# One semaphore or two for the turns of two kinds of products in a packed TensorE stream

## The chip, the cores and the metric

The kernel runs on one core of a Trainium2 chip. The metric is the device time of one execution in microseconds; three runs of the kernel before took 1469.01, 1470.53 and 1471.32 us, median 1470.53.

## The reference

Attention and a dense MLP work in parallel on the same normalised input, and both are added to the input. S = 2048 rows, D = 512, 32 heads of 16, F = 1792, all in f32.

```python
xn = _layernorm(x, axis=-1)
q, k, v = split(xn @ wqkv)                       # 32 heads of 16
p = softmax(einsum("bhqd,bhkd->bhqk", q, k) * 16 ** -0.5)
a = einsum("bhqk,bhkd->bhqd", p, v) -> (S, D) @ wo
m = gelu(xn @ w1 + b1) @ w2 + b2
out = x + a + m
```

## The kernel before, in words

**Units.** The attention is cut into 32 tasks (8 groups of 4 heads times 4 blocks of 512 queries) of 16 units each, 512 units in all. A unit does four score tiles twice: once as S, 128 queries by 512 keys, of which VectorE takes the row maxima (`s_half`, the `reduce_max` in line 366, tiles `pS`), and 19 units later (`LEAD`) once as T, 128 keys by 512 queries (`e_half`, tiles `pT`), of which ScalarE takes the exponentials (line 414, `pe<-pT`). The products of the exponentials with v (`v_half`, tiles `pV`, f32) follow one or two units behind. They add up over the 16 units of a task in one PSUM bank. A column of ones in v gives the softmax's sums.

**Dense work.** The projections of q, k and v, the MLP and the output projection are cut into groups (class `Group`), whose products add up in one PSUM bank too (tiles `pD`). f32 values are split into two f16 halves, and each product is made of three f16 products. `unit` takes from the current group a fixed number of them per half unit (`dense`): the pace (4, 4), (3, 4) or (3, 3), for even and odd units. The first MLP layer has 56 groups of 12 products on each side, (3, 3) for even and (4, 4) for odd f; the second has 16 groups of 42 products on each side, (3, 4) for the first eight and (4, 4) for the others. All else has (4, 4).

**Packing.** Scores, v products and dense products contract over at most 64 rows, and each is issued as four products of 64 rows by 32 columns. Such a product uses one of eight tiles of the TensorE array: one of two sides (partitions 0 to 63 or 64 to 127) and one of four columns of 32. I call four products that fill one side a set. Sets on the two sides run at the same time. Two sets that add up into one bank must not, so that V and D each change sides from half unit to half unit: where V is on one side, D is on the other, and in the next half unit they change places.

**The order of a half unit**, called a block here, is written out in `unit`: T, S, S, T (two on each side), then V (one set), then 3 or 4 sets of D, all on the other side than V. Only in the first block of a task D stands ahead of V. There are 1024 blocks with V. All instructions are issued in that order, with the manual schedule of line 863.

**Turns.** V of a block adds into the bank that V of the block before wrote from the other side, and so does D. To keep them apart, the last V product and the last D product of a block each count up a semaphore when they end (`leave`), unless their bank is finished with them. The first counted product of the next block waits for it (`enter` and `product`): V as a rule, since it stands ahead of D.

**Other waits** on TensorE: T waits until ScalarE has emptied its bank (three banks and one more shared with D), S until VectorE has (three banks), and a D product for its operands' DMA or for the GELU.

Of the kernel before, what the change touches and what calls it, by code (L numbers as in the profile page):

```python
# [54 lines left out]
def layer_kernel(ctx: ExitStack, tc: tile.TileContext, x, wqkv, wo, w1, b1, w2, b2, out):  # L55
# [63 lines left out]
    turn = [0]  # L119
# [41 lines left out]

    turns = tc.alloc_semaphore("turns")
    counted, left, newest, goal = [0], [], {}, [None]

    def product(user, *args, **kw):

        p = nc.tensor.matmul(*args, **kw)  # L169
        if user is None:  # L170
            return
        if goal[0] is not None:
            p._wait_ge(turns, counted[0])
            tc.declare_fence(p.ins, group=goal[0])
            goal[0] = None
        newest[user] = p

    def leave(user, goes_on):

        p = newest.pop(user, None)  # L180
        if p is not None and goes_on:
            p.then_inc(turns, 1)
            tc.no_tile_sem_insts.add(p.ins.name)
            counted[0] += 1
            left.append(p)

    def enter():

        if left:
            goal[0] = f"turn{counted[0]}"  # L190
            for p in left:
                tc.add_to_no_dep_group(goal[0], p.ins)
            left.clear()

    def tiled(user, dst, lhs, rhs, start, stop):

        for j in range(0, P, 32):
            product(user, dst[j:j + 32], lhs[:, j:j + 32], rhs, start=start, stop=stop)
# [218 lines left out]
    def v_half(u, a):  # L417

        t, kt = divmod(u, 16)
        g, qb = divmod(t, NQB)  # L420
        if kt == 0 and a == 0:
            pv_of[t] = hold("V", "S")
        pv = pv_of[t][0]
        r = slice(64 * a, 64 * a + 64)
        for h in (2, 3, 0, 1):
            c = (4 * g + h) * VW
            product("V", pv[32 * h:32 * h + 32, :], vv[r, kt, c:c + 32], ptiles[u, h][r],
                    start=(kt == 0 and a == 0), stop=(kt == 15 and a == 1))
# [321 lines left out]
    def land():  # L750

        settle()
        while extra[0] is not None:
            for side in range(2):
                if extra[0] is not None:
                    spare(None, side)
        if cur[0] is not None:
            enter()
        for side in range(2):
            while cur[0] is not None and cur[0].left(side):  # L760
                nc.tensor.drain()
                while cur[0].left(side):
                    cur[0].product(side)
        ended()

    def unit(gen):
# [7 lines left out]
        for a in range(2):  # L774
# [7 lines left out]
            if e >= 0:  # L782
                one_more()
                enter()

                w, r = (e - 2, 1) if a == 0 else (e - 1, 0)
                live = 0 <= w < NU
                new = r == 0 and w % 16 == 0
                if live and not new:
                    v_half(w, r)  # L790
                dense(gen, 1 - r)
                if live and new:
                    v_half(w, r)

                for user, goes_on in (("V", live and not (r == 1 and w % 16 == 15)),
                                      ("D", cur[0] is not None and not cur[0].over())):
                    leave(user, goes_on)
                for k in backlog:
                    backlog[k] = max(0, backlog[k] - HALF)
                if live and r == 1:  # L800
                    v_end(w)
                ended(False)
# [715 lines left out]
```

## Time and profile before

| | |
|---|---|
| median of three runs | 1470.53 us |
| the profiled execution, from first to last instruction | 1469.7 us |
| instructions | 88685, of them 40184 matmul records on TensorE |
| TensorE busy (any tile) | 1451.6 us, 99% |
| VectorE busy | 1368.7 us, 93% |
| ScalarE busy | 1259.3 us, 86% |
| GpSimd busy | 664.1 us, 45% |
| granted TensorE clock, mean | 0.996 |

Of the profiled execution no other time is given than its span; the median of the runs is 0.8 us above it. Times in the listings are microseconds. A timeline row gives start, duration, engine, line, operation, the tiles written and read, shapes and a count; rows of equal instructions that follow closely are merged, and the duration is then that of all of them. A row of a group gives the count, the busy time, the mean in ns of one, and the engine's idle time before them. An f32 product on TensorE stands in the trace as two records, one after the other. TensorE's matmul rows have modelled ends.

### The profile page before, as it was taken

What the parts mean: (1) busy time and instruction counts of PE and PEld (TensorE: products, weight loads), DVE (VectorE), ACT (ScalarE), POOL (GpSimd) and SP (SyncE); (2) the same over time, 40 slices, a digit from 0 to 9 for tenths busy, and PEclk for the clock granted to TensorE, in tenths of its full rate; (3) what the DMA queues carried; (4) which work ended last, traced back from release to release, by engine and by line L of the source; (5) the groups of instructions that cost most, each with busy time, mean ns of one, the idle gap of its engine ahead of it and who ended that gap; (6) DMA issues with size and microseconds to landing.
All of it is one profiled execution on the core that took longest, in us unless ns stands there. A gap on an engine that the chain in (4) does not pass through costs nothing.

```text
span 1469.7 us, 88685 instructions
## 1 busy us (share of the span) xinstructions
PE 1451.6 (99%) x40184; PEld 838.7 (57%) x40184; DVE 1368.7 (93%) x2304; ACT 1259.3 (86%) x2367; POOL 664.1 (45%) x673
## 2 busy tenths in 40 slices
PE   7999999999999999999999999999999999999998
PEld 3446556565565555556555556565555656555554
DVE  6989999999999999999999999999999999999933
ACT  5868888888999888899988889998889999888885
POOL 3201857554778411288740138883105777121110
PEclk9999999999999999999999999999999999999999
DMA  6731465455224211221113011121112210121423
GB/s 212 222 124 54 147 200 179 146 177 151 83 69 130 65 32 29 59 71 42 44 44 87 25 43 44 46 82 44 44 37 70 61 38 20 52 61 46 128 73 117
DMA packets 112627, 124.86 MB, mean 85 GB/s; under 512 B 22908, under 2 KB 84220, under 8 KB 112248
## 3 DMA queue, kind: packets, MB, share of 16 engines
q1 hardware_dynamic: 112248, 119.18, 26.6%
q8 instruction: 314, 5.14, 1.4%
q14 instruction: 65, 0.53, 0.1%
HBM read 81.66 MB, written 37.34 MB: 81 GB/s over the span
## 4 chain that ended last, share of the span: by engine, by line
PE 95%; DVE 2%; ACT 1%; DMA 1%; issue 1%; SPq 0%; DVEq 0%; ACTq 0%
PE pV L169 28%; PE pD L169 27%; PE pT L169 20%; PE pS L169 18%; PE pT L1015 2%; DMA wq<-in_A_wqkv_dram 1%; DVE mt L366 1%; PE pD L1015 1%; ACT xs L968 0%; ACT pe L414 0%; DVE ac L1393 0%; ACT wqk_h L904 0%; DVE xt L998 0%; DMA out_dram<-ac 0%; PE pT L985 0%
## 5 line engine op out<-in xcount | busy, mean ns | idle before, releaser
L366 DVE TENSOR_REDUCE mt<-pS 128x1 f32<-128x512 f32 x2029 | 1292.3, 684 | 39.2 <-PE pS L169 8.3
L414 ACT ACTIVATE pe<-pT 128x512 f32<-128x512 f32 x2048 | 1109.8, 599 | 166.5 <-PE pT L169 98.3
L169 PE MATMUL pV<-pe,vv 64*32 64x512 f32 x8192 | 1080.5, 595 | 0.1
L169 PE MATMUL pT<-qst,kst 64*32 64x512 f16 x8192 | 709.0, 377 | 2.1 <-issue 1.7
L169 PE MATMUL pS<-kst,qst 62*32 62x512 f16 x8116 | 590.2, 378 | 2.6 <-DVE mt L366 2.0
L169 PEld LDWEIGHTS <-qst 62*32 62x32 f16 x8192 | 292.0, 91 | 239.8 <-issue 42.4
L169 PE MATMUL pD<-xb,wc 64*32 64x512 f16 x5376 | 360.8, 376 | 0.0
L169 PE MATMUL pD<-w_s,g 64*32 64x512 f16 x5376 | 357.1, 377 | 0.0
L169 PEld LDWEIGHTS <-kst 64*32 64x32 f16 x8192 | 269.6, 91 | 115.8 <-issue 26.8
L169 PEld LDWEIGHTS pV<-pe,vv 64*32 64x32 f32 x8192 | 182.3, 105 | 85.6 <-PE pV L169 4.9
L169 PE MATMUL pD<-xt,wqk_h 64*32 64x512 f16 x2400 | 158.5, 377 | 0.3 <-issue 0.3
L169 PEld LDWEIGHTS <-wc 64*32 64x32 f16 x5376 | 123.2, 91 | 47.2 <-issue 0.5
L169 PEld LDWEIGHTS <-g 64*32 64x32 f16 x5376 | 118.2, 92 | 40.7
L1360 POOL TENSOR_TENSOR xa<-xa,yt 128x512 f32<-128x512 f32 x16 | 20.5, 1280 | 227.4 <-ACT yt L1358 227.4
L471 POOL TENSOR_TENSOR osb<-osb,rb 128x512 f32<-128x512 f32 x31 | 39.8, 1285 | 157.3 <-DMA rb<-den_d 133.9
L1312 POOL TENSOR_TENSOR t<-hh 128x512 f32<-128x512 f32 x56 | 58.2, 1039 | 82.3 <-ACT hh L1335 81.2
L1314 POOL TENSOR_TENSOR t<-t,hh 128x512 f32<-128x512 f32 x56 | 71.8, 1282 | 4.7
L1307 POOL TENSOR_TENSOR t<-t,hh 128x512 f32<-128x512 f32 x56 | 71.7, 1281 | 4.7
L169 PEld LDWEIGHTS <-wqk_h 64*32 64x32 f16 x2400 | 57.2, 92 | 22.0 <-issue 3.2
L1309 POOL TENSOR_TENSOR g<-t,g 128x512 f16<-128x512 f32 x56 | 65.2, 1165 | 4.7
L1306 POOL TENSOR_SCALAR t<-t,gs 128x512 f32<-128x512 f32 x56 | 38.8, 693 | 59.2 <-ACT t L1301 59.2
L169 PE MATMUL pD<-wo_s,oc 64*32 64x512 f16 x816 | 54.1, 377 | 0.0
(165 smaller groups left out, 880.9 us busy)
## 6 DMA issues: line engine op xcount, KB each, us to landing
wc<-w_d SPq DMA_DIRECT2D x56, 256.0 KB
qk_d<-stg SPq DMA_DIRECT2D x32, 256.0 KB
rb<-den_d SPq DMA_DIRECT2D x124, 64.0 KB
wch<-in_B_w_dram SPq DMA_DIRECT2D x14, 512.0 KB
wch<-in_B_w_dram SPq DMA_DIRECT2D x28, 256.0 KB
w_d<-wsp SPq DMA_DIRECT2D x28, 256.0 KB
kst<-qk_d SPq DMA_DIRECT2D x64, 96.0 KB
qst<-qk_d SPq DMA_DIRECT2D x64, 96.0 KB
```

The costliest lines, as they stand in the source:

```text
L169: p = nc.tensor.matmul(*args, **kw)
L366: nc.vector.reduce_max(mt_of[t][:, n, qt, kb:kb + 1], s, axis=AX.X)
L414: nc.scalar.activation(pe, st, AF.Exp, scale=scale_of[g // 2])
L471: pooled((1280, lambda: nc.gpsimd.tensor_tensor(osb, osb, rb, op=ALU.mult)), (620, lambda: nc.gpsimd.tensor_scalar(ot[:, 0], osb, 1.0, 0.0 ...
L1015: nc.tensor.matmul(tl[key], lhs, rhs, start=c + n == 0, stop=(c, n) == (NC - 1, 2))
L1306: pooled((690, lambda: nc.gpsimd.tensor_scalar(t1, t1, 1.0, gs[:, 1:2], op0=ALU.add, op1=ALU.mult)), (1280, lambda: nc.gpsimd.tensor_tenso ...
L1307: (1280, lambda: nc.gpsimd.tensor_tensor(t1, t1, hh, op=ALU.mult)),
L1309: (1160, lambda: nc.gpsimd.tensor_tensor(g[:, 1, f, :], t1, g[:, 0, f, :], op=ALU.subtract)),
L1312: pooled((1040, lambda: nc.gpsimd.tensor_tensor(t1, hh, hh, op=ALU.mult)), (620, lambda: nc.gpsimd.tensor_scalar(t1, t1, 1.0, 1.0 / GELU_A ...
L1314: (1280, lambda: nc.gpsimd.tensor_tensor(t1, t1, hh, op=ALU.mult)),
L1360: add = lambda: nc.gpsimd.tensor_tensor(xa, xa, yt, op=ALU.add)
```

## The change

The one semaphore for both kinds becomes a pair, and so do the count, the list of products that count, and the number to wait for. A block's first V product waits for the count of the V products alone, and its first D product for that of the D products alone.

```diff
-    turns = tc.alloc_semaphore("turns")
-    counted, left, newest, goal = [0], [], {}, [None]
+    turns = {u: tc.alloc_semaphore(f"turns{u}") for u in "VD"}
+    counted, left, newest, goal = {u: 0 for u in "VD"}, {u: [] for u in "VD"}, {}, {}
...
-        if goal[0] is not None:
-            p._wait_ge(turns, counted[0])
-            tc.declare_fence(p.ins, group=goal[0])
-            goal[0] = None
+        if user in goal:
+            p._wait_ge(turns[user], counted[user])
+            tc.declare_fence(p.ins, group=goal.pop(user))
         newest[user] = p
...
-            p.then_inc(turns, 1)
+            p.then_inc(turns[user], 1)
             tc.no_tile_sem_insts.add(p.ins.name)
-            counted[0] += 1
-            left.append(p)
+            counted[user] += 1
+            left[user].append(p)
...
-        if left:
-            goal[0] = f"turn{counted[0]}"
-            for p in left:
-                tc.add_to_no_dep_group(goal[0], p.ins)
-            left.clear()
+        for user, ps_ in left.items():
+            if ps_:
+                goal[user] = f"turn{user}{counted[user]}"
+                for p in ps_:
+                    tc.add_to_no_dep_group(goal[user], p.ins)
+                ps_.clear()
```

No instruction changes its place on any engine; the waits on TensorE change. In the second MLP layer, before, the stream from the last T product of a block to its first D products reads as follows (`kst` is a stack of keys, here the weights of T; `g` is the GELU's output, the weights of D):

```order
L169 MATMUL pT<-qst_3_90,kst_2_81 32x512
L169 MATMUL pV<-pe,vv 32x512 [waits turns]
L169 MATMUL pV<-pe,vv 32x512 x3
L169 LDWEIGHTS g
L169 MATMUL pD<-w_s,g 32x512
```

And at the same place of the changed kernel:

```order
L169 MATMUL pT<-qst_3_90,kst_2_81 32x512
L169 MATMUL pV<-pe,vv 32x512 [waits turnsV]
L169 MATMUL pV<-pe,vv 32x512 x3
L169 LDWEIGHTS g
L169 MATMUL pD<-w_s,g 32x512 [waits turnsD]
```

The first D product now has a wait, behind the four V products and its own weight load; V's wait has changed its semaphore.

## The prediction

> **What bounds the kernel now.** I read the page first, for the engines' busy shares and the chain that ended last; then the groups of instructions by form, for how often and how long each kind runs; then the timeline of TensorE in three places, for what a block waits for; last, the timelines of VectorE, for how close it is to its own limit.
>
> The page gives the shares of the span:
>
> ```profile
> PE 1451.6 (99%) x40184; PEld 838.7 (57%) x40184; DVE 1368.7 (93%) x2304; ACT 1259.3 (86%) x2367; POOL 664.1 (45%) x673
> PE 95%; DVE 2%; ACT 1%; DMA 1%; issue 1%; SPq 0%; DVEq 0%; ACTq 0%
> ```
>
> The chain lies on TensorE for 95% of the span, but 99% busy says little: eight products run side by side in the array's eight tiles (two sides of 64 rows, four columns of 32), and the row counts as busy while any of them runs. Whether time is lost shows only in when each set starts. The groups say how many there are:
>
> ```profile
> L366 DVE TENSOR_REDUCE mt<-pS 128x1 f32<-128x512 f32 x2029 | 1292.3, 684 | 39.2 <-PE pS L169 8.3 <-PE pT L169 6.8 <-PE pV L169 2.3
> ...
> L169 PE MATMUL pV<-pe,vv 64*32 64x512 f32 x8192 | 1080.5, 595 | 0.1
> ...
> L169 PE MATMUL pD<-xb,wc 64*32 64x512 f16 x5376 | 360.8, 376 | 0.0
> L169 PE MATMUL pD<-w_s,g 64*32 64x512 f16 x5376 | 357.1, 377 | 0.0
> ...
> L169 PE MATMUL pD<-xt,wqk_h 64*32 64x512 f16 x2400 | 158.5, 377 | 0.3 <-issue 0.3
> ...
> L169 PE MATMUL pD<-wo_s,oc 64*32 64x512 f16 x816 | 54.1, 377 | 0.0
> ...
> L169 PE MATMUL pD<-wvh,xt 64*32 64x512 f16 x480 | 31.4, 377 | 0.0
> ...
> L169 PE MATMUL pD<-wo_s,xb 64*32 64x512 f16 x336 | 22.7, 377 | 0.0
> ```
>
> The V products are f32 and stand in the trace as two records each: 8192 records are 4 products in each of 1024 blocks. The dense products number 5376 + 5376 + 2400 + 816 + 480 + 336 = 14784, or 3696 sets of four. By the paces in the code, groups of the pace (3, 3) (28, each of 24 sets) take 8 blocks of 3 sets, 224 blocks in all; groups of the pace (3, 4) (8, each of 84 sets) take 24 blocks, half of them of 3 sets: 96. So 320 blocks have 3 sets, and the other 3696 - 960 = 2736 sets fill 684 blocks of 4.
>
> Now one block of 3 sets and the next one's start, in TensorE's timeline (start, duration in us; x8 is two sets):
>
> ```profile
> 622.13 0.63 PE L169 MATMUL pV<-pe,vv 64*32 64x512 f32 x4
> 622.18 0.61 PE L169 MATMUL pD<-xb,wc 64*32 64x512 f16 x8
> 622.59 0.61 PE L169 MATMUL pV<-pe,vv 64*32 64x512 f32 x4
> 622.61 0.39 PE L169 MATMUL pD<-xb,wc 64*32 64x512 f16 x4
> 622.83 0.39 PE L169 MATMUL pT<-qst,kst 64*32 64x512 f16 x4
> 623.02 0.42 PE L169 MATMUL pS<-kst,qst 62*32 62x512 f16 x8
> 623.24 0.40 PE L169 MATMUL pT<-qst,kst 64*32 64x512 f16 x4
> 623.41 0.63 PE L169 MATMUL pV<-pe,vv 64*32 64x512 f32 x4
> 623.46 0.61 PE L169 MATMUL pD<-xb,wc 64*32 64x512 f16 x8
> ...
> 624.69 0.63 PE L169 MATMUL pV<-pe,vv 64*32 64x512 f32 x4
> ```
>
> An f16 set holds its side for 0.22 us (two start in 0.61 - 0.39). The side with D was free after 3 D sets, one T and one S: 622.18 + 5 x 0.215 = 623.26. That is the side of the next V, and it starts only at 623.41: 0.15 us late. Its own forerunner ended at 622.59 + 0.61 = 623.20, so V starts 0.21 after that. The D products, by their rows, had ended at 623.00. What V waited for is told by another place, where a dense group ends, so that its last D products are not counted and only V's are:
>
> ```profile
> 608.98 0.63 PE L169 MATMUL pV<-pe,vv 64*32 64x512 f32 x4
> ...
> 609.43 0.61 PE L169 MATMUL pV<-pe,vv 64*32 64x512 f32 x4
> ...
> 610.13 0.63 PE L169 MATMUL pV<-pe,vv 64*32 64x512 f32 x4
> 610.30 0.61 PE L169 MATMUL pD<-xb,wc 64*32 64x512 f16 x8
> ...
> 610.73 0.61 PE L169 MATMUL pD<-xb,wc 64*32 64x512 f16 x8
> ...
> 611.60 0.61 PE L169 MATMUL pV<-pe,vv 64*32 64x512 f32 x4
> ```
>
> Here V starts 0.09 after its forerunner's end (609.43 + 0.61 = 610.04), a period of 1.15 us where the counted block took 1.28. So the D count arrives some 0.12 us after the V count, though the D rows end earlier: the next V waits for it. That is the gate which the change takes away.
>
> By the rows' ends alone the D count would cost nothing and the change would save nothing in these blocks. The Trainium skill (TensorE: Matmul & The Clock Gate, Part 3, "The mechanism") says instead that matmuls end in the order of the program, so that D, standing behind V, cannot be told as ended before it; the 0.21 against 0.09 agrees with that rule and not with the ends that the rows give.
>
> **The change part by part.** It moves no instruction. *Counts*: the same two per block, on two semaphores instead of one; nothing. *V's wait* loses the D count; *D's first product* gets a wait of its own, for a count that V waited for a moment before. Behind it in TensorE's stream stand the block's other D products and the next block's T and S, for which ScalarE and VectorE wait. A wait that is already met shows no cost: the eight S products at 623.02 hold two waits and start within 0.42 - 0.38 = 0.04 us. I take 0 for it. From above it is bounded by the 0.09 from an end to a start, if it comes last; from below a gain is excluded, since a wait adds nothing.
>
> What is late once the gate is gone is the side. V(n+1) follows D(n) on its side, D(n+1) follows V(n). From V to the next block's D the first listing takes 623.46 - 622.13 = 1.33. From D to the next V, 3 sets take 5 x 0.215 = 1.08, and 4 sets 6 x 0.215 = 1.30; the second listing has 611.60 - 610.30 = 1.30 for 4. A pair of 3-set blocks then takes 1.33 + 1.08 = 2.41, not 2.56 (624.69 - 622.13): 0.075 less per block. D itself starts no earlier in the first such block: the gain comes through the V that starts earlier and lets the D after it start earlier.
>
> Blocks of 4 sets are already held by their sides:
>
> ```profile
> 591.98 0.63 PE L169 MATMUL pV<-pe,vv 64*32 64x512 f32 x4
> 592.02 0.61 PE L169 MATMUL pD<-w_s,g 64*32 64x512 f16 x8
> ...
> 593.32 0.39 PE L169 MATMUL pD<-w_s,g 64*32 64x512 f16 x2
> 593.33 0.59 PE L169 MATMUL pV<-pe,vv 64*32 64x512 f32 x1
> ...
> 594.63 0.62 PE L169 MATMUL pV<-pe,vv 64*32 64x512 f32 x4
> 594.64 0.40 PE L169 MATMUL pD<-w_s,g 64*32 64x512 f16 x4
> ```
>
> D to V is 1.31 twice, V to D 1.34 and 1.31; two blocks take 2.65 and by their sides 1.31 + 1.31 = 2.62, so at most 0.015 a block is there to gain.
>
> VectorE is next in line. It takes four reductions per unit (two blocks):
>
> ```profile
> 618.42 8.93 DVE L366 TENSOR_REDUCE mt<-pS 128x1 f32<-128x512 f32 x14
> 728.71 1.28 DVE L366 TENSOR_REDUCE mt<-pS 128x1 f32<-128x512 f32 x2
> ```
>
> and, in the groups, its small operations that return with every 16 units:
>
> ```profile
> L458 DVE RECIPROCAL dn<-dn 64x32 f32<-64x32 f32 x31 | 10.4, 334 | 0.0
> L382 DVE TENSOR_REDUCE mneg<-mt 128x16 f32<-128x64 f32 x31 | 6.8, 220 | 1.1
> ```
>
> Back to back one costs 1.28 - 0.684 = 0.60, while a run of 14 without a visible gap goes at (8.93 - 0.684) / 13 = 0.634: the 93% busy hides 5% of slack. Two reductions and the small operations (17 us in these two groups over 1024 blocks, 0.02) make 1.22 per block. That is above the 1.205 of the 3-set pair, so VectorE takes over there and the saving is 1.275 - 1.22 = 0.055.
>
> The sum:
> - Groups of the pace (3, 3): 28 x 7 blocks (the eighth's D is not counted today either) x 0.055 = 10.8 us; by the sides alone 14.7.
> - Groups of the pace (3, 4): 48 times two blocks of 3 and two of 4. Today 2.56 + 2.65 = 5.21; then 1.33 + 1.08 + 1.31 + 1.30 = 5.02: 0.19, in all 9.1 us. VectorE's 4 x 1.22 = 4.88 leaves room.
> - The other 684 - 96 = 588 blocks of 4: x 0.015 = 8.8 us at most.
>
> All of it is 32.6 us by the sides. I don't take all: some blocks are late for another reason (ScalarE's release of a T bank, a group's new bank), and a V that may start earlier gains nothing there. I choose two thirds for the first two, since most periods around the listings are regular, and half for the third, whose 0.015 is near what the rows resolve: 7.2 + 6.1 + 4.4 = 17.7 us. The profiled execution's span is 1469.7 us and the median of the runs 1470.5, 0.8 above; the saving lies within the span, so 1470.5 - 17.7 gives 1453.
>
> **The rivals.**
> - *The evacuation holds it* (0.13). VectorE's 98% in the middle is real after all, or ScalarE's T banks come no sooner, and a V that starts early only waits for tiles that follow late; or D's count is not the gate that the listings make of it. For it: one row of 680 us,
>
> ```profile
> 340.00:1020.00 680.00, 679.09 (x19704) 401.05 (x19692) 668.24 (x1101) 608.04 (x1148) 357.90 (x366) 1.00 0.21 62
> ```
>
> with 668 of 680 us on VectorE. Against it: the 0.634 against 0.60. If the 0.634 were its real pace, two reductions and 0.02 are 1.29 per block, above today's 1.28, and nothing is gained: 1468 to 1473. The Trainium skill (TensorEngine Tiling (Array Packing), "PSUM Bottleneck") speaks for it: packing speeds up TensorE, not the emptying of PSUM, which may become the bound. By that rule the time stays.
> - *D's own wait comes late* (0.09), on the other side. In blocks of 4, D now waits behind V, and its count comes last; T and S of the next block stand behind it. If D starts 0.05 after its side is free (half of the 0.09 from an end to a start), 684 blocks lose 34 us; less the 13.3 of the first two terms that is 21 slower, 1491. It decides from 13.3 / 684 = 0.02 per block on. Against it: the D count lets a product start 1.28 after V (that is today's period with 3 sets), and the side is free only at 1.31 to 1.33, so the wait is met 0.03 to 0.05 before it matters. For it: a fourth set makes the count later, and may use up that margin.
> - *All of it and more* (0.12): the sides run free of each other, and the stalls by ScalarE are absorbed too: 32.6 us or over, 1438 and below, say 1430.
>
> My forecast has the remaining 0.66. A time within 0.2% (3 us) of the time before counts as the same, about what a measurement of this kernel can tell; faster is 0.66 + 0.12 = 0.78, the same 0.13, slower 0.09. The range runs from 1440, nearly all of the 32.6, to 1470, where nothing is gained; the slower rival and half of the larger gain are left out.
>
> **What would show it.** After the change, in a group of the pace (3, 3): V to V alternating near 1.15 and 1.25, its mean 1.20 to 1.23 where it was 1.28; D to its next V 1.08. V starts 0.09 after the end of the V before, D 0.15 or so after V, not 0.05. VectorE's long runs go at 0.61 instead of 0.634. Blocks of 4 stay at 1.30 to 1.32. Wrong would be: V early and the period still 1.28 with T or S waiting for ScalarE or VectorE (first rival), or D to V beyond 1.30 in blocks of 4 with idle sides (second).

## The result and the profile after

The changed kernel takes 1450.25 us (median of 4 runs, 1449.44 to 1452.72), the kernel before 1470.16 in the same comparison: a ratio of 0.9871, 95% interval 0.9855 to 0.9886. That is 19.9 us, where 17.7 were forecast (1453, range 1440 to 1470).

The page of the changed kernel has, for the busy shares and the chain that ended last:

```profile
PE 1432.0 (99%) x40184; PEld 964.6 (67%) x40184; DVE 1353.8 (93%) x2304; ACT 1255.9 (87%) x2367; POOL 663.8 (46%) x673
PE 87%; DVE 8%; DMA 2%; ACT 1%; issue 1%; SPq 0%; DVEq 0%; ACTq 0%
```

TensorE still reads 99% and VectorE 93%: these shares do not tell that anything changed. Two other figures do: the weight loads (PEld) go from 57% to 67%, of which no run looks for the cause, and VectorE has 8% of the chain where it had 2%. The products with v alone, in the window of 660 us in which most of the MLP runs, before:

```profile
340.00:1000.00 660.00, 531.08 (x4028) 86.71 (x4024) 0.00 (x0) 9.60 (x16) 1.00 0.21 61
```

and after:

```profile
340.00:1000.00 660.00, 543.33 (x4104) 115.16 (x4096) 0.00 (x0) 9.66 (x16) 1.00 0.21 61
```

The first count is TensorE's records: at eight a block, 503.5 blocks before and 513 after in the same time, 1.311 us a block and 1.287.

TensorE's timeline in a group of the pace (3, 3), after the change:

```profile
610.94 0.61 PE L169 MATMUL pV<-pe,vv 64*32 64x512 f32 x4
610.98 0.61 PE L169 MATMUL pD<-xb,wc 64*32 64x512 f16 x8
611.37 0.61 PE L169 MATMUL pV<-pe,vv 64*32 64x512 f32 x4
611.40 0.40 PE L169 MATMUL pD<-xb,wc 64*32 64x512 f16 x4
...
612.08 0.63 PE L169 MATMUL pV<-pe,vv 64*32 64x512 f32 x4
612.23 0.61 PE L169 MATMUL pD<-xb,wc 64*32 64x512 f16 x8
...
613.32 0.61 PE L169 MATMUL pV<-pe,vv 64*32 64x512 f32 x4
613.40 0.61 PE L169 MATMUL pD<-xb,wc 64*32 64x512 f16 x8
...
614.49 0.61 PE L169 MATMUL pV<-pe,vv 64*32 64x512 f32 x4
614.61 0.61 PE L169 MATMUL pD<-xb,wc 64*32 64x512 f16 x8
...
615.69 0.61 PE L169 MATMUL pV<-pe,vv 64*32 64x512 f32 x4
```

V now follows V after 1.14, 1.24, 1.17 and 1.20, where it was 1.28 each time. At 612.08 it starts 0.10 after the V before has ended (611.37 + 0.61 = 611.98): its wait is V's own. The other three start 0.13 to 0.17 after it, when their side is free. From D to the next V it is 1.10, 1.09, 1.09 and 1.08, the side's own time. D no longer starts with V but 0.04 to 0.15 behind it, because the two sides run at their own pace.

The traces also hold the times at which each semaphore counts up, and these show the gate itself. Before the change, 281 blocks behind a block of 3 sets find both counts. D's count comes 0.126 us after V's (median), and in 262 of the 281 V starts 0.044 to 0.047 after D's. After the change V starts that soon behind its own count in 59 of 313 blocks behind 3 sets; in the others it starts later.

Behind blocks of 4 sets V started so soon after D's count in only 93 of 580 blocks before the change; after it, V starts so soon behind its own count in 6 of 646.

A group of the pace (3, 4), two blocks of 4 sets and two of 3:

```profile
576.57 0.65 PE L169 MATMUL pV<-pe,vv 64*32 64x512 f32 x4
...
577.98 0.61 PE L169 MATMUL pV<-pe,vv 64*32 64x512 f32 x4
...
579.21 0.65 PE L169 MATMUL pV<-pe,vv 64*32 64x512 f32 x4
...
580.41 0.61 PE L169 MATMUL pV<-pe,vv 64*32 64x512 f32 x4
...
581.60 0.64 PE L169 MATMUL pV<-pe,vv 64*32 64x512 f32 x4
```

The four take 5.03 us; the prediction has 5.21 before and 5.02 after. This is one of the better places: all 48 such fours take 5.23 on average before and 5.12 after, a gain of 0.11 each and not 0.19. And VectorE, in the first of these two places:

```profile
607.83 10.55 DVE L366 TENSOR_REDUCE mt<-pS 128x1 f32<-128x512 f32 x17
```

A reduction every (10.55 - 0.684) / 16 = 0.617 us, where it was 0.634.

From the V starts of whole traces I grouped the periods by the number of sets in a block. Before, 323 blocks of 3 sets have a mean of 1.271 us and 669 of 4 sets 1.360; after, 1.229 and 1.351. The change is worth 0.042 for a block of 3 sets and 0.009 for one of 4: 323 x 0.042 + 669 x 0.009 = 13.6 + 6.0 = 19.6 us, nearly all of the 20.6 between the two profiled executions.

### The profile page after: what moved, and what is told of

The parts are those of the page before. It is cut to its first block, busy times and chain, and to the rows that moved or that the text cites. A ratio compares the mean times of both kernels' runs of the same rounds, so it can differ in the third digit from the quotient of the medians.

```text
span 1449.1 us, 88687 instructions
## 1 busy us (share of the span) xinstructions
PE 1432.0 (99%) x40184; PEld 964.6 (67%) x40184; DVE 1353.8 (93%) x2304; ACT 1255.9 (87%) x2367; POOL 663.8 (46%) x673
## 4 chain that ended last, share of the span: by engine, by line
PE 87%; DVE 8%; DMA 2%; ACT 1%; issue 1%; SPq 0%; DVEq 0%; ACTq 0%
PE pD L169 26%; PE pV L169 25%; PE pT L169 17%; PE pS L169 16%; DVE mt L366 7%; PE pT L1015 2%; DMA wq<-in_A_wqkv_dram 1%; PE pD L1015 1%; DMA m_d<-mhl 0%; ACT xs L968 0%; DVE xt L998 0%; ACT pe L414 0%; DMA qst<-m_d 0%; DVE ac L1393 0%; ACT wqk_h L904 0%
## 5 line engine op out<-in xcount | busy, mean ns | idle before, releaser
L366 DVE TENSOR_REDUCE mt<-pS 128x1 f32<-128x512 f32 x2029 | 1277.4, 682 | 34.8 <-PE pS L169 7.8
L169 PE MATMUL pS<-kst,qst 62*32 62x512 f16 x8116 | 627.0, 378 | 2.6 <-DVE mt L366 2.0
L169 PEld LDWEIGHTS <-qst 62*32 62x32 f16 x8192 | 309.3, 90 | 196.7 <-issue 50.9
L169 PE MATMUL pD<-w_s,g 64*32 64x512 f16 x5376 | 361.8, 375 | 0.0
L169 PEld LDWEIGHTS <-kst 64*32 64x32 f16 x8192 | 280.5, 91 | 96.0 <-issue 24.2
L169 PEld LDWEIGHTS pV<-pe,vv 64*32 64x32 f32 x8192 | 245.3, 105 | 13.6 <-PE pV L169 4.2
L169 PEld LDWEIGHTS <-wc 64*32 64x32 f16 x5376 | 160.7, 91 | 44.5 <-issue 0.4
L169 PEld LDWEIGHTS <-g 64*32 64x32 f16 x5376 | 163.5, 91 | 39.2 <-issue 0.5
L169 PEld LDWEIGHTS <-wqk_h 64*32 64x32 f16 x2400 | 74.0, 92 | 19.9 <-issue 2.0
```

The source lines that it names most:

```text
L366: nc.vector.reduce_max(mt_of[t][:, n, qt, kb:kb + 1], s, axis=AX.X)
```

## The experiments

The theory: V waited for a D count that comes 0.12 us after V's own; blocks of 3 sets, whose sides are free earlier than that, give most of the gain; a wait that is already met costs nothing. The main rival: what counts is the number of pairs of waits that are taken apart, whatever the block, less what the second wait costs. Times below are medians of their own comparison; the kernel before stands at 1469.47, 1468.07 and 1469.85 us in the three of them.

**The second wait alone.**

```diff
...
+        elif user == "D" and again[0] is not None:
+            p._wait_ge(turns, again[0])
...
```

The lines left out note down the number to wait for in `again`.

> One semaphore as before, V's wait for both counts as before; D's first product waits once more, for the same count that V ahead of it has just waited for. So it has the changed kernel's second wait in every block (1895 waits against 1026) but not V's earlier release. Theory (the gain is V's release from the late D count, and a wait already met costs nothing): 1470 us as before, within 2. Rival (a second wait in the stream costs time, which the changed kernel pays and more than earns back): above 1475; at half of the 0.09 us from an end to a start, 869 waits would cost 39 us, 1509.

Measured: 1470.19 us, ratio 0.9999 (0.9989 to 1.0008). Some 870 more waits on TensorE, each already met, cost nothing that can be measured: at most 0.0008 x 1470 = 1.2 us, 1.4 ns a wait. The changed kernel's second wait is not the same, though: it is for a count of its own, which comes after V's. Its trace has the time between that count and D's start. A product that is held by a count starts 0.044 after it; D starts at a median of 0.053 after its count behind blocks of 4 sets (within 0.047 in 4 of 603) and 0.088 behind blocks of 3 (in 28 of 286). So there too the wait is met nearly always, by 0.01 us in the blocks of 4, and the rival's loss does not show.

**Apart only after blocks of 3 sets, and only after blocks of 4.** One edit, with `TIED = 4` and `TIED = 3`:

```diff
...
+        first = "V" if tied[0] and "V" in goal else user
...
+        if user == "D" and made_d[0] == 4 * TIED:
+            user = "V"
+            tied[0] = True
...
```

> Two semaphores as in the changed kernel, but after a block of 4 dense sets D counts on V's semaphore, so that the next block's first product waits for both as before. Only after blocks of 3 sets (or fewer) are the waits apart. Theory: the gain sits in the 3-set blocks, whose sides are free 0.15 us before the D count; 13 to 14 of the 20 us stay, 1456 to 1457. Rival (each separated pair of waits is worth the same, whatever the block): about 290 of 900 pairs are apart, a third of the gain, 1463 to 1464.

> The counterpart: after blocks of 3 sets the next block's first product waits for both as before, after blocks of 4 the waits are apart. Theory: the 4-set blocks are held by their sides and give 0.009 us each, about 6 us in all: 1464. Rival (each pair is worth the same): about 610 of 900 pairs are apart, two thirds of the gain, 1457.

Measured: 1456.44 us apart after 3 sets, ratio 0.9913 (0.9900 to 0.9926), and 1464.74 apart after 4, ratio 0.9966 (0.9953 to 0.9979). So a third of the pairs gives 13.0 us, and the other two thirds give 4.7. The rival had it the other way round and falls. The two ratios multiplied give 0.9879, within the interval of the whole change.

**The same change at other paces.** The base has one semaphore, its counterpart two.

```diff
-FAST, MEAN, SLOW = (4, 4), (3, 4), (3, 3)
+FAST, MEAN, SLOW = (4, 4), (3, 3), (3, 3)
```

> One semaphore as before; the second MLP layer's first eight groups get the pace (3, 3) in place of (3, 4): 448 blocks of 3 sets and 553 of 4, where there were 321 and 670. It is the base for the next kernel and is compared with it; its own time against before is open (the same dense work, later: 1465 to 1480).

> The same pace with two semaphores. Theory (0.042 us for a block of 3 sets, 0.009 for one of 4, as the traces before and after the change have them): 448 x 0.042 + 553 x 0.009 = 23.8 us below the kernel with this pace and one semaphore. Rival (every pair of waits that is taken apart is worth the same, 20 us / 903 = 0.022): as many pairs as before, 20 to 22 us.

and with (4, 4) in the place of (3, 4):

> One semaphore; the same eight groups at the pace (4, 4): 227 blocks of 3 sets, 743 of 4. Base for the next kernel; its own time against before is open (1465 to 1480).

> The same pace (4, 4) with two semaphores. Theory: 227 x 0.042 + 743 x 0.009 = 16.2 us below the kernel with this pace and one semaphore, so some 7 us less than at the pace (3, 3). Rival (each pair is worth the same): 20 to 22 us, as at the pace (3, 3).

Measured at (3, 3): 1477.91 and 1454.67 us, 23.2 apart (theory 23.8, rival 20 to 22). At (4, 4): 1469.28 and 1454.75, 14.5 apart (theory 16.2, rival 20 to 22). Each kernel's ratio to before is known to about 0.0015, some 2 us, and a difference of two to some 3 us. So the first pair does not part theory from rival; the second does, and the rival falls by it. The worth of the change follows the number of 3-set blocks. Neither pace beats the changed kernel's 1450.

**D ahead of V.**

```diff
-                if live and not new:
-                    v_half(w, r)
                 dense(gen, 1 - r)
-                if live and new:
+                if live:
                     v_half(w, r)
```

> One semaphore as before, but D stands ahead of V in every block, not only in the first of a task. Theory (counts arrive in the order of the stream, so that what stands last is counted last): V's count now comes last and D's costs nothing beside it. The block's first wait ends at 1.15 us after the V before, D's side is free only at 1.32, and V follows behind the issue of 3 or 4 D sets (0.08 to 0.1): a 3-set pair at 1.20 to 1.25 us per block instead of 1.28, and much of the gain without a second semaphore, 1452 to 1462. Rival (the D count is late by itself, by how many products it stands for): periods stay at 1.28, 1468 to 1472.

Measured: 1473.34 us, ratio 1.0025 (1.0016 to 1.0035): slower than before, outside both expectations. A stretch of 4-set blocks in its TensorE timeline says why:

```profile
1040.18 0.39 PE L169 MATMUL pD<-w_s,g 64*32 64x512 f16 x4
1040.22 0.63 PE L169 MATMUL pV<-pe,vv 64*32 64x512 f32 x4
...
1041.04 0.40 PE L169 MATMUL pT<-qst,kst 64*32 64x512 f16 x4
1041.10 0.56 PE L169 MATMUL pS<-kst,qst 62*32 62x512 f16 x8
1041.32 0.40 PE L169 MATMUL pT<-qst,kst 64*32 64x512 f16 x4
1041.54 0.40 PE L169 MATMUL pD<-w_s,g 64*32 64x512 f16 x4
1041.57 0.63 PE L169 MATMUL pV<-pe,vv 64*32 64x512 f32 x4
...
1042.89 0.39 PE L169 MATMUL pD<-w_s,g 64*32 64x512 f16 x4
1042.92 0.63 PE L169 MATMUL pV<-pe,vv 64*32 64x512 f32 x4
```

The side of the next V is free after T and S, 1041.04 + 2 x 0.22 = 1041.48, but V starts at 1041.57, 0.03 behind D, whose side is free only at 1041.32 + 0.22 = 1041.54. So every block takes V to D, 1.32, and 0.03 more: 1.35, where the sides took turns at 1.31 before. In 3-set blocks the theory's gain is there (pairs at a mean of 1.250 instead of 1.277), but 4-set blocks are twice as many. Whether V's count, which D waits for here, holds D back, or the place in the stream holds V back, this run left open. Two semaphores tell it:

> D ahead of V in every block, as in the run with one semaphore that came out at 1473, but with two. There the 4-set blocks took 1.354, with V starting 0.03 after D although its side was free 0.09 before. Theory A (the order of the stream does it: V waits in the stream until D's first set has its side, 1.32 after the V before): 4-set blocks stay at 1.35, 1465 to 1473. Theory B (V's count, which D waits for there, does it): the separate counts take it away, 1448 to 1455.

Measured: 1465.63 us, ratio 0.9979 (0.9967 to 0.9990), between before and the change. The same place:

```profile
1041.32 0.39 PE L169 MATMUL pD<-w_s,g 64*32 64x512 f16 x4
1041.36 0.63 PE L169 MATMUL pV<-pe,vv 64*32 64x512 f32 x4
...
1042.68 0.39 PE L169 MATMUL pD<-w_s,g 64*32 64x512 f16 x4
1042.71 0.63 PE L169 MATMUL pV<-pe,vv 64*32 64x512 f32 x4
```

V still starts 0.03 to 0.04 behind D, and the period is still 1.35 (1041.36 to 1042.71). Neither product is held by its count: behind blocks of 4 sets V starts at a median of 0.22 after V's count and D 0.28 after D's, where a product that is held starts 0.044 after. So it is the order of the stream: V waits until D's first set has its side. With V ahead D is not held back alike: in the 4-set listing of before, D starts at 593.32 and V, which stands ahead of it, at 593.33.

This run also tells why the D count was late. With D ahead of V, D's count comes before V's in blocks of 3 and 4 sets (0.092 us or more), and 0.02 to 0.04 after the row of its last product ends. In the changed kernel, with V ahead, it comes 0.28 after that row's end in blocks of 3 sets (median). So it is D's place behind V that makes its count late.

**Half of VectorE's work.**

```diff
-        nc.vector.reduce_max(mt_of[t][:, n, qt, kb:kb + 1], s, axis=AX.X)
+        nc.vector.reduce_max(mt_of[t][:, n, qt, kb:kb + 1], s[:, 0:QB // 2], axis=AX.X)
```

> One semaphore; VectorE takes the row maximum over 256 of the 512 columns of each S tile, so half of that work is left out (what is subtracted ahead of the exponential is then the maximum of half the keys). VectorE's part of a block falls from 2 x 0.60 to about 2 x 0.33 us. Theory (the D count's gate and the sides of the array set the pace before): the 3-set blocks stay at 1.28 and the 4-set ones at 1.31; only stalls shrink, 1455 to 1468. Rival (VectorE is what the kernel before runs at): well below, 1420 or less.

> The same halved maxima with two semaphores. The prediction has VectorE take over in blocks of 3 sets at 1.22 us, above the 1.205 of the sides. If that is so, the 3-set pairs fall from 1.231 to about 1.205 and the change is worth more here, up to the 32.6 us by the sides: 25 to 32 us below the kernel with halved maxima and one semaphore. If VectorE does not hold them, the change is worth 18 to 21 us, as with whole maxima.

A reduction takes 419 ns with half the columns, where it took 684. Measured: 1462.76 us with one semaphore, ratio 0.9956 (0.9942 to 0.9970), and 1442.09 with two, ratio 0.9816 (0.9803 to 0.9830). The change is worth 20.7 us here, as much as with whole maxima: VectorE does not hold it. How idle VectorE is then is seen in the waits, with one semaphore (engine, line, waited for: us in total, times, longest):

```profile
DVE mt L366 <- PE pT L169: 275.6, 498, 1.6
DVE mt L366 <- PE pS L169: 249.9, 471, 4.9
```

and with two:

```profile
DVE mt L366 <- PE pS L169: 310.1, 603, 4.9
...
DVE mt L366 <- PE pT L169: 195.1, 355, 1.6
```

It waits over 500 us for TensorE in both. The 1442 are the shortest time of all runs, but with work left out; of the versions with all the work, the changed kernel stays the fastest.

Pairs of neighbouring blocks with equal sets, mean period of a block in us, from the V starts of each trace:

| kernel | 3 sets | 4 sets |
|---|---|---|
| before | 1.277 | 1.357 |
| after | 1.231 | 1.346 |
| second wait alone | 1.279 | 1.356 |
| apart after 3 sets only | 1.231 | 1.355 |
| apart after 4 sets only | 1.279 | 1.348 |
| half maxima, one semaphore | 1.269 | 1.349 |
| half maxima, two | 1.219 | 1.343 |
| D ahead, one semaphore | 1.250 | 1.367 |
| D ahead, two | 1.238 | 1.360 |

Each row is one profiled execution; that of D ahead with one semaphore took 1478.14 us, 4.8 above its kernel's median. The means change by up to 0.004 with the rule by which D sets are given to blocks, and so do the 0.042 and 0.009 above (0.040 and 0.010 by another rule).

## Why the prediction was right, step by step

- *The gate is the D count.* Right. The two runs with the waits apart in one kind of block only put the gain where this step puts it, and in the trace before V starts 0.044 to 0.047 behind the second of the two counts in 262 of 281 blocks behind 3 sets. That the count is late by its place behind V, as the prediction argued, is shown by the two semaphores with D ahead.
- *A wait already met costs nothing.* Right: 0.9999.
- *The sides take over, at 1.205 in 3-set blocks.* Right for a block that nothing else holds: the listing after has 1.14 to 1.24, on average (615.69 - 610.94) / 4 = 1.19, and the median of all 322 blocks of 3 sets in the trace after is 1.205. V to D is 1.29 and 1.32 in the listing, not 1.33 throughout.
- *VectorE takes over from the sides at 1.22.* This step failed. The stretch above and the median lie below 1.22, and with half the maxima the change is worth the same. So the 1.22 is no bar in each block; that the three S banks even it out is likely, but no run tried it. The mean of the 322 blocks, 1.231, lies above the median by a few late ones: 29 take 1.30 or more and the other 293 have a mean of 1.207, so that the 29 cost 7.9 us. In 24 of the 29 a T starts within 0.05 of a count of ScalarE (14) or an S within 0.05 of one of VectorE (15). With half the maxima and two semaphores there are 21 such blocks, none with an S behind VectorE, and they cost 3.6 us. So VectorE costs a 3-set block time in a few late places and not in each; leaving out ScalarE's work was not tried.
- *Today's block at 1.275.* The saving 1.275 - 1.22 starts from 1.275 where the prediction's own listing has 1.28; this makes 0.7 us in the sum.
- *The sum, term by term.* Blocks outside the pace (3, 4), with 3 sets: 7.2 in the sum, 7.4 between the two traces. The fours of the pace (3, 4): 6.1 in the sum, 5.1 measured; 5.02 a four was forecast, the listing has 5.03 but the mean of all 48 is 5.12. The other blocks of 4: 4.4 in the sum, 6.9 measured, 0.012 a block where half of at most 0.015 was taken; the sum has 588 of them, the traces 575.
- *Two thirds of the 3-set blocks.* That the first term came out is luck in part: 0.055 by VectorE x 2/3 = 0.037 a block was in the sum, and the failed step and the choice nearly cancelled. With the sides' 0.075 and the 0.042 measured for all blocks of 3, a little over half of the gain came, and not two thirds.
- *The rival that D's own wait comes late.* It did not: 4-set pairs went down, from 1.357 to 1.346. But it was close: a fourth set makes D's count 0.033 later, and the margin of 0.03 to 0.05 that the prediction has for it is 0.01 in the trace after (0.053 against 0.044). The rival of the evacuation falls with the half maxima, and the larger gain of 32.6 us did not come even then (20.7).

## What to carry to other kernels

Two chains of products that each have to wait for their own forerunner should not share a count: the later of the two ends then gates both, even where the rows show its products done first. A busy share of 99% hides such a wait; two places in the timeline, one with the count and one without, show it. And what a removed wait is worth is read per kind of block, from when the next resource (here a side of the array) comes free.

## What the runs showed that was not expected

- The D count's distance from V's is a fixed step. In the trace after, where the two counts are apart, the semaphore events put D's count 0.126 us after V's in blocks of 3 sets (275 times) and 0.159 in blocks of 4 (552 times): 0.033 a set, 8 ns for each further product that stands behind V, although the D rows of the 3-set blocks end 0.1 to 0.2 before V's (611.40 + 0.40 against 611.98 in the first block of the listing after). Counts come in the order of the stream: with D ahead and two semaphores, it is V's count that comes behind, 0.092 after D's in the blocks of 4. The Trainium skill (TensorE: Matmul & The Clock Gate, Part 3, "The mechanism") has matmuls end in the order of the program; these counts agree with that.
- A product with a free side does not pass one that stands ahead of it and waits for its side: with four sets of D ahead, V starts 0.03 after D's first, not 0.06 before it (1041.57 against 1041.54 and 1041.48).
- Taking half of VectorE's largest piece of work away gains 7.1 us (1469.85 to 1462.76) on a kernel in which VectorE reads 93% busy.
